# Attention into a two-layer block: the first batch's second layer takes three output chunks at once, and its weight pieces come later and closer together

## The chip, the cores and the metric

The kernel runs on one core of a Trainium2 chip. A core has a matrix engine (PE), a vector engine (DVE), a scalar engine (ACT), GpSimd (POOL) and a queue engine (SP) that here issues nearly all transfers (DMA). Each engine works through its own instructions in the order of the program; semaphores make one wait for another. The metric is the device time of one execution in microseconds (us).

## The reference

Eight batches of 12 heads with 448 positions of 64 numbers go through attention with normalized queries and keys; the result is bridged to 3584 rows of 768 and goes through two matrix products with an activation between them.

```python
q_n, k_n = (rmsnorm(q, g_q), rmsnorm(k, g_k))
scores = scale * np.matmul(q_n, k_n.transpose(0, 1, 3, 2))
attn = softmax(scores)                      # written out in the reference, with 1e-9 in the sum
x = np.matmul(attn, v)                      # then (B, H, S, D) -> (B*S, H*D)
h = x @ w_in                                # 768 -> 2048
g = h - np.tanh(h)
out = g @ w_out                             # 2048 -> 768
```

`w_in` and `w_out` arrive as float64, so the kernel reads each weight as two 32-bit words and rounds it itself.

## The kernel before

**Slots.** Attention goes by pairs of heads: six pairs in each of eight batches, 48 slots. In one slot the kernel computes the values of pair s and the scores of pair s + 1, and prepares pairs s + 2 and s + 3. Slots 0 to 5 (`first_slot`) hold attention of batch 0 alone, beside the first weights. Slots 6 to 11 (`early_slot`) hold attention of batch 1 and, woven between its parts, both layers of batch 0. From slot 12 on (`slot`) each batch's layers run beside a later batch's attention. The layers are a Python generator, `mlp`; `run(ns)` lets it emit matmuls worth so many ns between two parts of attention. In slots 6, 7 and 8 the first layer of batch 0 is emitted, 56 matmuls of 224 columns in each; in slots 9, 10 and 11 its second layer (`project_first`), 32 matmuls of 448 columns in each. One such matmul is two PE instructions in the profile.

In `early_slot` the order is: totals and two score chunks of the next pair, matmuls, the turning of a later pair's keys and queries, matmuls, the last score chunk, the values, the third score chunk, then four stretches of matmuls with the sums of exponentials, the norms and the query scaling between them. From `HALVED` on, which is slot 11, it is another: `visit` weaves the values of pair s with the scores of pair s + 1 in one block, with the score banks cut from five to three and two banks kept for the values.

**First layer.** It is done in blocks of a scheme that needs seven products where eight would be plain (`products`): four sets (j) of seven products (p, in `ORDER`), each with a weight block that is either a part of `w_in` or a sum of such parts. For batch 0 these parts are made just in time. The later batches read them back from DRAM, where the kernel keeps them.

**Pieces.** A weight piece is 128 x 768 weights, 768 KB as it arrives. Pieces 0 to 15 are `w_in`, 16 to 31 `w_out`. A piece goes through five steps on five engines: `weight_load` (L290 or L294, SP) into one of three raw buffers, `round_weight_a` (L71, L72, ACT), `round_weight_b` (L78, L79, L82, DVE), `round_weight_c` (L92, POOL), and `keep_w_out` (L388, SP), which writes some of them to DRAM. `weight(to)` emits ACT's step of the pieces below `to`, and the DVE and POOL steps of the piece before; `place_free` lets piece n be loaded only when piece n - 3 has finished on POOL. The list `due` says how many pieces must have been emitted at each of the 28 products; `combine` adds up blocks of `w_in` on DVE (L357).

**Second layer of batch 0.** `project_first` computes the six output chunks of 128 columns one after the other, 16 matmuls each, in one of three banks (`mm`). In the first three chunks it emits the last eight pieces, one in every six matmuls. In the last three chunks it emits `combine_w_out` (L381 to L384, DVE), which makes sums of `w_out` blocks for the later batches, one in every four matmuls, with their writing to DRAM (`late["keep"]`, L388). A finished chunk is copied by ACT (L1345), turned by DVE (L966) and stored by four transfers (L971), which `step_out` releases. `ring_load` brings the next batch's weight blocks into a ring of six slots.

**What the other parts do.** `norm_q` scales queries, on ACT in eight pieces (L454) for the pairs 9 to 12 and on DVE in one (L456) for others. `totals` multiplies the exponentials' sums with ones on PE (L700) and takes the reciprocal on DVE (L705); in `visit` it takes an `mm` bank, elsewhere in these slots an `sc` bank. `scores` puts two heads' scores into two `sc` banks, which are free for the next user once ACT has taken their exponentials (L575).

Of the kernel before, what the change touches and what calls it, by code (L numbers as in the profile page):

```python
# [147 lines left out]
def bounded_path(tc, ctx, q, k, v, moe_w_in, moe_w_out, out, g_col, ident, ones, half_ones, neg_half, early):  # L148
# [17 lines left out]
    nc = tc.nc  # L166
    B, H, S, D = q.shape
    DFF, DM = moe_w_out.shape
    P = 128
# [45 lines left out]
    def mm_bank():  # L215
        return bank_of("mm")
# [48 lines left out]
    def w_out_row(f, i):  # L265
        return w_half[i][f // 2][:, f % 2]
# [54 lines left out]
    def weight(to):  # L321

        while done[1] < min(to, PIECES):
            n = done[1]
            keep_step(0, {CF - 4: 0, CF: 1, CF + HF: SETS - 1}.get(n, -1))
            round_weight_a(nc, raws[n], weight_dst(n))
            settle(n)
            done[1] = n + 1
            load_weights(n + (3 if n < EARLY - 3 else 4))
            if kept[1] < kept[0] and n >= 4 * kept[0] + 2:  # L330
                keep_weights()
            keep_step(2)
        if done[1] == PIECES:
            settle(PIECES)
# [40 lines left out]
    def combine_w_out(f):  # L375

        a11, a21 = (w_out_row(f, i) for i in range(2))
        a12, a22 = (w_out_row(f + HF, i) for i in range(2))
        t = [ring_slot() for _ in range(2)]
        s3, s1, s2, s4 = (t[i // 2][:, i % 2 * HALF : (i % 2 + 1) * HALF] for i in range(4))  # L380
        nc.vector.tensor_tensor(out=s1, in0=a21, in1=a22, op=ALU.add)  # L381
        nc.vector.tensor_tensor(out=s3, in0=a11, in1=a21, op=ALU.subtract)
        nc.vector.tensor_tensor(out=s2, in0=s1, in1=a11, op=ALU.subtract)
        nc.vector.tensor_tensor(out=s4, in0=a12, in1=s2, op=ALU.subtract)  # L384
        late["keep"].append(lambda: [keep_factors(3 + 2 * i, 2, f, t[i]) for i in range(2)])

    def keep_factors(n, count, f, src):
        nc.sync.dma_start(  # L388
            out=w_out_dram[:, n : n + count, :, f, :].rearrange("p k c d -> p (k c) d"),
            in_=src[:, : count * HALF].rearrange("p (k d) -> p k d", d=P),  # L390
        )

    def keep_w_out(n):

        if not CF <= n < PIECES:
            return
        f, i, src = weight_piece(n)
        if f >= HF or i == 0:
            blk = i + 1 if f >= HF else 0
            for r in range(2):  # L400
                keep_factors(blk, 1, f % HF + r, src[:, r])
# [18 lines left out]
    def ring_load(to):  # L420

        for n in range(len(ring_tiles), min(to, len(ring_steps))):
            b, layer, j, p = ring_steps[n]
            t = ring_tiles[ring_steps[n]] = ring_slot()
            if layer == 0:
                assert kept[1] > j
                nc.sync.dma_start(out=t[:, : 2 * HALF], in_=w_in_dram[j, p])
            elif layer == 2 and p == 0:
                nc.sync.dma_start(out=t, in_=w_out_dram[:, BLOCKS[j], HC - 1].rearrange("p f d -> p (f d)"))
            elif layer == 2:  # L430
                n = min(2 * HB, 7 * HB - 2 * (p - 1) * HB)
                at = 2 * (p - 1) * HB
                nc.sync.dma_start(out=t[:, :n], in_=inner_dram[j][:, at : at + n])
            else:
                nc.sync.dma_start(out=t, in_=w_out_dram[:, BLOCKS[p], j].rearrange("p f d -> p (f d)"))
# [11 lines left out]
    def norm_q(s):  # L447
        rr, n = normed[s], early["n"]
        t = loaded.pop(("q", s))
        if NP + 3 <= s < 2 * NP + 1:  # L450
            for h in range(2):
                for c in range(NCH):
                    i = h * NCH + c
                    nc.scalar.mul(n[:, c, h], t[:, h, c], rr[:CP, 1, i : i + 1])  # L454
            return
        nc.vector.tensor_tensor(  # L456
            out=n.rearrange("p c h d -> p h c d"), in0=t,
            in1=rr[:CP, 1].rearrange("p (h c) -> p h c", h=2)[:, :, :, None].to_broadcast([CP, 2, NCH, D]),
            op=ALU.mult,
        )  # L460
# [91 lines left out]
    def sc_bank():  # L552
        return bank_of("sc")
# [93 lines left out]
    def visit(s, av):  # L647

        wave(*half_values(s, 2, av, True))
        for c in range(2):  # L650
            v0, v1 = half_values(s, c, av, False)
            if has(s + 1):
                (s0, exp0), (s1, exp1) = scores(s + 1, c, True)
                wave(s0, v1)
                exp0()
                wave(v0, s1)
                exp1()
            else:
                wave(v0, v1)
        last_values(s, av)  # L660
        del loaded["v", s]
        if s >= FOLDED:
            divide(s, av)
        if has(s + 1):
            scores(s + 1, 2)
        if s < FOLDED:
            totals(s, mm_bank())
            divide(s, av)

    def values(s, av, chunks=(2, 0, 1)):  # L670
# [14 lines left out]
    def totals(s, dn):  # L685

        parts = [t[:, h, n * HS : (n + 1) * HS] for t in sums.get(s, ()) for n in range(2) for h in range(2)]
        parts = [(parts, [ones[:, :BL]] * 2)] if parts else []
        if not sums.pop(s):
            for p in full(s):  # L690
                parts.append(
                    ([p[:, h, n * HS : (n + 1) * HS] for n in range(2) for h in range(2)], [ones[:, :BL]] * 2)
                )
            last = probs[s, KF]
            parts.append(([last[:, h, 0] for _ in range(2) for h in range(2)], [half_ones[:, n] for n in range(2)]))
        for i, (moving, by) in enumerate(parts):
            for n in range(2):
                for h in range(2):
                    r = (2 * n + h) * BL
                    nc.tensor.matmul(  # L700
                        dn[r : r + BL, :HS], lhsT=by[n], rhs=moving[2 * n + h],
                        start=(i == 0), stop=(i == len(parts) - 1),
                    )
        rs = whole[s] = sp.tile([P, HS], F32, name="rs")
        nc.vector.reciprocal(rs, dn[:, :HS])  # L705


    HALVED, FOLDED = 2 * NP - 1, 2 * NP + 1

    def fold(s):  # L710

# [100 lines left out]
    late = {}  # L812


    due = [EARLY + (CF - EARLY) * (m + 1) // (7 * SETS // 2) for m in range(7 * SETS // 2)]
    due += [CF + HF * (m + 1) // (7 * SETS // 2) for m in range(7 * SETS // 2)]
    assert len(due) == 7 * SETS and due[-1] == CF + HF

    def part(name):
        if name == "th" and "blocks" in late:  # L820
# [189 lines left out]
    def step_out(by=1):  # L1010
        for entry in late["out"]:
            entry[0] -= by
        while late["out"] and late["out"][0][0] <= 0:
            late["out"].pop(0)[1]()
# [294 lines left out]
    def project_first(b):  # L1309

        g = late["g"]
        for fn in late["todo"]:
            fn()
        late["todo"] = []
        keep_step(0, SETS - 1)
        took = 4 * S / ENGINE_NS
        for m in range(CD * CF):
            k, f = m // CF, m % CF
            n = (k + HC) % CD
            if f == 0:  # L1320
                bank = mm_bank()
            if f == CF // 2:
                step_out(2)
            if k < HC:
                weight(CF + HF + HF * (m + 1) // (HC * CF))
            elif m < HC * CF + 2:
                keep_w_out(PIECES - 2 + m - HC * CF)
            elif (m - HC * CF) % 4 == 0 and m - HC * CF <= 4 * HF:
                for fn in late["keep"]:
                    fn()  # L1330
                late["keep"] = []
                combine_w_out((m - HC * CF) // 4 - 1)
            elif m == CD * CF - 12:
                ring_load(2)
                for fn in late["keep"]:
                    fn()
            elif m == CD * CF - 10:
                ring_load(4)
            nc.tensor.matmul(  # L1339
                bank[:, :S], lhsT=w_out_row(f, n // HC)[:, n % HC * P : (n % HC + 1) * P], rhs=g[:, f, :],  # L1340
                start=(f == 0), stop=(f == CF - 1),
            )
            if f == CF - 1:
                y = part("s2").rearrange("p f s -> p (f s)")
                nc.scalar.copy(out=y, in_=bank[:, :S])  # L1345
                store(b, n, y)
            yield took
        wp_stack.close()
        late["blocks"] = pool("blocks", bufs=1)
        late["second"] = pool("second", bufs=1)  # L1350
        late["tg"] = single_stack.enter_context(tc.tile_pool(name="tg", bufs=1))
        late["inner"] = inner_steps()
# [527 lines left out]
```

## Time and profile before

| what | value |
|---|---|
| median of three runs | 1344.18 us (1344.12 to 1344.48) |
| profiled execution | 1342.53 us |
| its span, first to last instruction | 1340.7 us |
| PE, DVE, ACT, POOL busy | 1311.5, 969.5, 568.1, 795.0 us |
| mean granted PE clock | 0.998 |
| slots 6, 7, 8 (first layer of batch 0) | 36.67, 33.16, 30.28 us |
| slots 9, 10, 11 (second layer of batch 0) | 32.90, 31.70, 31.03 us |

A slot's length is taken from the start of its first PE group to that of the next slot. In a line of a timeline the columns are the start, the length, the engine, the line of the kernel, the operation, what it writes and reads, shape and count; the bracket says how long the engine had been idle before it and what ended that. A line of the waits has who waited for whom, the total in us, how often, and the longest. A busy engine is one with an instruction in flight; PE's ends are modelled, so its 98% is not 98% of its peak.

### The profile page before, as it was taken

Reading aid. Unit: us, or ns where it says so; the run is one execution under the profiler, and the core shown is the slowest. Engines: PE = TensorE matmul, PEld = TensorE weight load, DVE = VectorE, ACT = ScalarE, POOL = GpSimd, SP = SyncE. Lnnn points to the kernel's source line nnn. Section 1 sums busy time; section 2 is a strip of 40 time slices with the busy share of each in tenths; the row PEclk is TensorE's granted clock in tenths of the full one; section 3 lists DMA queues with packets and bytes.
Section 4 is the critical chain, followed back from the end, with each engine's and each line's share of the span. In section 5 each row is a group of like instructions: output and inputs, shape, how many; then the busy total and the mean of one; then the engine's idle time right before and its main releaser. Section 6 shows DMA issues by size and latency. Waiting matters only on the chain.

```text
span 1340.7 us, 29301 instructions
## 1 busy us (share of the span) xinstructions
PE 1311.5 (98%) x11368; PEld 1033.4 (77%) x11368; DVE 969.5 (72%) x1410; ACT 568.1 (42%) x1328; POOL 795.0 (59%) x591
## 2 busy tenths in 40 slices
PE   7989999999999999999999999999999999999997
PEld 3467854488998888688878788779887888799986
DVE  4999978867765767688888576768888667634455
ACT  7856654244343454445322445454512254311102
POOL 4766776348846256726698245944699244812771
PEclk9999999999999999999999999999999999999999
DMA  7779889889999766476655867466745776466544
GB/s 169 183 214 262 265 260 231 250 278 279 340 284 287 181 160 180 112 186 155 171 149 136 201 162 183 117 170 165 181 132 145 150 201 161 118 161 172 170 142 102
DMA packets 364759, 253.53 MB, mean 189 GB/s; under 512 B 273028, under 2 KB 303300, under 8 KB 364612
## 3 DMA queue, kind: packets, MB, share of 16 engines
q1 hardware_dynamic: 364608, 251.57, 69.1%
q8 instruction: 92, 1.51, 0.5%
q14 instruction: 55, 0.45, 0.1%
q10 hardware_dynamic: 4, 0.00, 0.0%
HBM read 205.23 MB, written 46.27 MB: 188 GB/s over the span
## 4 chain that ended last, share of the span: by engine, by line
PE 83%; DVE 7%; POOL 4%; DMA 2%; SPq 2%; issue 2%; ACT 1%; DVEq 0%; ACTq 0%; POOLq 0%
PE mm L857 38%; PE mm L1142 21%; PE sc L569 9%; PE sc L635 6%; PE mm L1339 5%; POOL u L1099 3%; PE sc L623 1%; POOL rr_mine L523 1%; PE sc L677 1%; DVE w_out L357 1%; PE mm L677 1%; SPq L497 1%; DVE rs L705 1%; DMA w_f<-w_inner 1%; DVE w_out L82 0%
## 5 line engine op out<-in xcount | busy, mean ns | idle before, releaser
L857 PE MATMUL mm<-xT,w_f 128*128 128x224 f32 x1296 | 263.5, 353 | 0.8 <-DVE xT L767 0.8
L857 PEld LDWEIGHTS mm<-xT,w_f 128*128 128x128 f32 x1296 | 244.8, 190 | 5.5 <-issue 4.2
L569 PE MATMUL sc<-qT,kT 64*32 64x448 f32 (+1 forms) x3072 | 215.6, 499 | 2.7 <-ACT p_last L575 2.1
L857 PE MATMUL mm<-tt,w_f 128*128 128x224 f32 x1044 | 212.6, 355 | 0.2 <-DMA w_f<-w_in 0.2
L857 PEld LDWEIGHTS mm<-tt,w_f 128*128 128x128 f32 x1044 | 195.8, 190 | 15.9 <-issue 15.4
L523 POOL TENSOR_TENSOR rr_mine<-rr_mine,neg_half 128x28 f32<-128x28 f32 x33 | 162.2, 4915 | 2.7
L762 DVE TENSOR_TENSOR xT<-xT,sc 128x448 f32<-128x448 f32 x34 | 21.0, 618 | 165.8 <-PE sc L569 114.8
L1142 PE MATMUL mm<-u,w_f 128*128 128x224 f32 x672 | 137.2, 354 | 1.0 <-POOL u L1099 0.5
L905 POOL TENSOR_TENSOR gT<-s,th 128x448 f32<-128x448 f32 x44 | 57.8, 1313 | 132.2 <-ACT th L904 128.7
L1142 PE MATMUL mm<-gT,w_f 128*128 128x224 f32 (+3 forms) x512 | 132.0, 412 | 1.2 <-DVE acc L1149 0.9
L1142 PEld LDWEIGHTS mm<-u,w_f 128*128 128x128 f32 x672 | 126.1, 190 | 8.0 <-POOL u L1099 3.6
L569 PEld LDWEIGHTS sc<-qT,kT 64*32 64x32 f32 x3072 | 72.4, 106 | 68.1 <-issue 49.2
L1142 PEld LDWEIGHTS mm<-gT,w_f 128*128 128x128 f32 x512 | 93.9, 190 | 34.3 <-issue 32.0
L635 PE MATMUL sc<-p,v_nat 64*32 64x448 f32 x1184 | 116.9, 536 | 0.0
L1142 PE MATMUL mm<-g,w_f 128*128 128x224 f32 (+1 forms) x360 | 98.9, 428 | 0.0
L575 ACT ACTIVATE p<-sc 128x448 f32<-128x448 f32 x132 | 71.9, 545 | 50.3 <-PE sc L569 37.4
L905 POOL TENSOR_TENSOR g<-s,th 128x448 f32<-128x448 f32 x24 | 30.3, 1264 | 105.1 <-ACT th L904 105.1
L1142 PEld LDWEIGHTS mm<-g,w_f 128*128 128x128 f32 x360 | 67.9, 190 | 26.5 <-issue 26.0
L729 ACT COPY sum_g<-sum 32x14 f32<-32x14 f32 x280 | 56.3, 201 | 72.0 <-DVE sum L721 66.3
L1339 PE MATMUL mm<-gT,w_out 128*128 128x448 f32 x192 | 74.0, 542 | 0.0
L145 POOL TENSOR_TENSOR rr<-rr,neg_half 112x8 f32<-112x8 f32 (+1 forms) x30 | 49.8, 1689 | 35.5 <-DVE rr L144 35.0
L1099 POOL TENSOR_TENSOR u<-gT 128x448 f32<-128x448 f32 x48 | 63.5, 1342 | 11.1 <-PE mm L1142 11.1
(206 smaller groups left out, 2465.8 us busy)
## 6 DMA issues: line engine op xcount, KB each, us to landing
w_f<-w_in SPq DMA_DIRECT2D x196, 384.0 KB, 3.5
w_f<-w_inner SPq DMA_DIRECT2D x63, 512.0 KB, 3.7
w_f<-w_out SPq DMA_DIRECT2D x42, 512.0 KB, 3.9
w_raw<-in_moe_w_out_dram SPq DMA_DIRECT2D x16, 768.0 KB, 5.4
w_in<-w_out SPq DMA_DIRECT2D x21, 384.0 KB, 5.3
qk_nat<-in_q_dram SPq DMA_DIRECT2D x132, 56.0 KB, 2.6
qk_nat<-in_k_dram SPq DMA_DIRECT2D x132, 56.0 KB, 2.4
g<-w_out SPq DMA_DIRECT2D x14, 512.0 KB, 5.4
```

The source lines that it names most:

```text
L145: nc.gpsimd.tensor_tensor(out=r, in0=r, in1=neg_half[:rows], op=ALU.pow)
L523: nc.gpsimd.tensor_tensor(out=mine, in0=mine, in1=neg_half[:, :1].to_broadcast([P, 2 * NJ]), op=ALU.pow)
L569: nc.tensor.matmul(tiles[h][i * BL : (i + 1) * BL, :n], lhsT=kT[r, c * P + at : c * P + at + BL], rhs=qT[r, first : first + n], start=True ...
L575: nc.scalar.activation(p[:, h, c if c < 2 else 0, :], tiles[h][:, :n], AF.Exp, scale=1.0 if rr is None else rr[:, 0, 2 * c + h : 2 * c + h ...
L635: nc.tensor.matmul(av[g][i * BL : (i + 1) * BL, :S], lhsT=v_nat[keys, h, c, m * BL : (m + 1) * BL], rhs=p[keys, h], start=first, stop=True ...
L677: nc.tensor.matmul(av[n][r : r + BL, :HS], lhsT=v_nat[:, h, c, m * BL : (m + 1) * BL], rhs=p[c][:, h, n * HS : (n + 1) * HS], start=False, ...
L729: nc.scalar.copy(out=acc[h * BL : (h + 1) * BL, g], in_=part[g * BL : (g + 1) * BL, h * NJ : (h + 1) * NJ])
L857: nc.tensor.matmul(bank[:, f * HS : (f + 1) * HS], lhsT=w[:, c * width + f, :], rhs=moving[p](c), start=(first and f == 0 and c == 0), sto ...
L905: eng.tensor_tensor(out=g[:, rows, cols], in0=h, in1=th, op=ALU.subtract)
L1099: nc.gpsimd.tensor_tensor(out=u[:, half], in0=a[:, half], in1=z[:, half], op=ALU.subtract)
L1142: nc.tensor.matmul(bank[:, :n], lhsT=w(i), rhs=mv, start=(first and i == 0), stop=(i == len(moving) - 1), skip_group_check=not first,)
L1339: nc.tensor.matmul(bank[:, :S], lhsT=w_out_row(f, n // HC)[:, n % HC * P : (n % HC + 1) * P], rhs=g[:, f, :], start=(f == 0), stop=(f == C ...
```

## The change

- `due` is one straight line: from 8 pieces at products 0 to 2 to 22 at product 27, where it went to 16 by product 13 and to 24 by product 27.
- `project_first` has its loops turned: it works on three chunks at once, in three banks, so that each third matmul belongs to the same chunk. The order of the halves stays.
- Ten pieces (22 to 31) are left for it. They are emitted in its first 32 matmuls, in the list `behind`.
- `combine_w_out` is emitted from matmul 24 on, one in every six matmuls, where it began at matmul 52 with one in four; for the last two of the eight, the writing to DRAM is cut into four transfers instead of two.
- Outputs are released by one step every four matmuls. The three chunks end within three matmuls, are copied into three buffers, and the third is turned into a buffer of another name.
- Ring loads are emitted at matmuls 80 and 84, where they were at 84 and 86.
- `HALVED` is slot 10, so slot 10 has the one visit too. `totals` in a visit takes an `sc` bank, since all three `mm` banks are in use.
- `norm_q` of pair 12 goes to DVE.

```diff
-        late["keep"].append(lambda: [keep_factors(3 + 2 * i, 2, f, t[i]) for i in range(2)])
+        if f < HF - 2:
+            late["keep"].append(lambda: [keep_factors(3 + 2 * i, 2, f, t[i]) for i in range(2)])
+            return
+        late["keep"].append(lambda: [keep_factors(3 + n, 1, f, s) for n, s in enumerate((s3, s1, s2, s4))])
...
-        if NP + 3 <= s < 2 * NP + 1:
+        if NP + 3 <= s < 2 * NP:
...
-            totals(s, mm_bank())
+            totals(s, sc_bank())
...
-    HALVED, FOLDED = 2 * NP - 1, 2 * NP + 1
+    HALVED, FOLDED = 2 * NP - 2, 2 * NP + 1
...
-    due = [EARLY + (CF - EARLY) * (m + 1) // (7 * SETS // 2) for m in range(7 * SETS // 2)]
-    due += [CF + HF * (m + 1) // (7 * SETS // 2) for m in range(7 * SETS // 2)]
-    assert len(due) == 7 * SETS and due[-1] == CF + HF
+    SOON_OUT, LAST_OUT = HF - 2, 32
+    due = [EARLY + (CF - EARLY + SOON_OUT) * max(m - 1, 0) // (7 * SETS - 2) for m in range(7 * SETS)]
+    behind = [min(PIECES, CF + SOON_OUT + (PIECES - CF - SOON_OUT) * (m + 1) // LAST_OUT) for m in range(CD * CF)]
+    assert due[-1] == CF + SOON_OUT and due[7 * (SETS - 1) - 1] > CF
...
-        for m in range(CD * CF):
-            k, f = m // CF, m % CF
-            n = (k + HC) % CD
-            if f == 0:
-                bank = mm_bank()
-            if f == CF // 2:
-                step_out(2)
-            if k < HC:
-                weight(CF + HF + HF * (m + 1) // (HC * CF))
-            elif m < HC * CF + 2:
-                keep_w_out(PIECES - 2 + m - HC * CF)
-            elif (m - HC * CF) % 4 == 0 and m - HC * CF <= 4 * HF:
+        combined = [0]
+
+        def keep_combined(to):
+            for f in range(combined[0], min(to, HF)):
                 for fn in late["keep"]:
                     fn()
                 late["keep"] = []
-                combine_w_out((m - HC * CF) // 4 - 1)
-            elif m == CD * CF - 12:
-                ring_load(2)
+                combine_w_out(f)
+                combined[0] = f + 1
+
+        for m in range(CD * CF):
+            k, f, i = m // (HC * CF), m % (HC * CF) // HC, m % HC
+            n = (1 - k) * HC + i
+            if m % 4 == 3:
+                step_out()
+            weight(behind[m])
+            if f == 0:
+                bank = [] if i == 0 else bank
+                bank.append(mm_bank())
+            if LAST_OUT <= m < LAST_OUT + 2:
+                keep_w_out(PIECES - 2 + m - LAST_OUT)
+            if m >= CF + HF:
+                keep_combined((m - CF - HF) // 6 + 1)
+            if m == CF + HF + 6 * HF:
                 for fn in late["keep"]:
                     fn()
-            elif m == CD * CF - 10:
+                late["keep"] = []
+            if m == CD * CF - 16:
+                ring_load(2)
+            elif m == CD * CF - 12:
                 ring_load(4)
             nc.tensor.matmul(
-                bank[:, :S], lhsT=w_out_row(f, n // HC)[:, n % HC * P : (n % HC + 1) * P], rhs=g[:, f, :],
+                bank[i][:, :S], lhsT=w_out_row(f, n // HC)[:, n % HC * P : (n % HC + 1) * P], rhs=g[:, f, :],
                 start=(f == 0), stop=(f == CF - 1),
             )
             if f == CF - 1:
-                y = part("s2").rearrange("p f s -> p (f s)")
-                nc.scalar.copy(out=y, in_=bank[:, :S])
-                store(b, n, y)
+                y = part(("s2", "s5", "s1")[i]).rearrange("p f s -> p (f s)")
+                nc.scalar.copy(out=y, in_=bank[i][:, :S])
+                store(b, n, y, part("s2").rearrange("p f s -> p (f s)") if i == 2 else None)
```

Here `NP` is 6, `CF` 16, `HF` 8, `CD` 6, `HC` 3, `SETS` 4, `EARLY` 8 and `PIECES` 32.

## The prediction, made before the change was run

> **What bounds the kernel now.** I read the page first: who is busy, and how the matrix clock stands.
>
> ```profile
> span 1340.7 us, 29301 instructions
> PE 1311.5 (98%) x11368; PEld 1033.4 (77%) x11368; DVE 969.5 (72%) x1410; ACT 568.1 (42%) x1328; POOL 795.0 (59%) x591
> ```
>
> PE is idle for 29.2 us of the span, so the change can gain only where PE stands still, or by taking work from PE. Next I cut the stretch that the change touches into slots 6 to 11, by the starts of their first PE groups, and asked for the busy time of each (us, then PE, PEld, DVE, ACT, POOL, granted clock, DMA share, GB/s):
>
> ```profile
> 72.83:109.50 36.67, 32.10 (x284) 25.99 (x277) 35.79 (x52) 19.02 (x30) 21.82 (x17) 0.95 0.84 229
> 109.50:142.66 33.16, 30.84 (x282) 25.44 (x281) 30.96 (x40) 19.82 (x37) 21.89 (x17) 1.00 0.92 261
> 142.66:172.94 30.28, 30.28 (x282) 25.50 (x281) 28.51 (x43) 18.12 (x35) 24.30 (x18) 1.00 0.84 255
> 172.90:205.80 32.90, 32.90 (x237) 16.35 (x236) 25.57 (x30) 19.79 (x36) 23.05 (x19) 1.00 0.83 258
> 205.78:237.48 31.70, 31.70 (x209) 15.55 (x209) 28.07 (x40) 15.63 (x30) 18.61 (x18) 1.00 0.95 244
> 237.48:268.51 31.03, 31.03 (x209) 15.39 (x208) 24.42 (x43) 8.08 (x15) 10.62 (x8) 1.00 0.84 245
> ```
>
> Slots 8 to 11 have no idle PE; slots 6 and 7 have 4.57 and 2.32 us, with DVE full. What PE waits for there, in the view of waits (slots 6 to 8):
>
> ```profile
> PE sc L467 <- DVE rs L705: 3.9, 2, 2.3
> PE mm L857 <- DVE s L926: 2.5, 1, 2.5
> PE mm L857 <- DVE rs L705: 0.5, 1, 0.5
> ```
>
> So DVE's backlog is the limit in slots 6 and 7, and PE alone from slot 8 on. Last, how a weight piece travels: ACT (L71, L72), DVE (L78 to L82), POOL (L92), and only then SP may load the piece three further on into the same raw buffer. One whole round, of piece 18 to piece 21, and two later waits, from the timeline (start, us):
>
> ```profile
> 152.00 0.90 ACT L71 ACTIVATE w_out<-w_raw 128x768 f32<-128x768 f32 x1
> 152.94 0.56 DVE L78 TENSOR_SCALAR w_out<-w_out 128x768 f32<-128x768 f32 x1 [0.41 <-ACT w_out L71]
> 156.05 2.62 POOL L92 TENSOR_TENSOR w_out<-w_out,w_raw 128x384 int32<-128x384 int32 x2
> 158.71 0.38 SPq L294 DMA_DIRECT2D w_raw<-in_moe_w_out_dram  x1
> 164.49 0.92 ACT L71 ACTIVATE w_out<-w_raw 128x768 f32<-128x768 f32 x1 [1.03 <-DMA w_raw<-in_moe_w_out_dram]
> ...
> 206.28 0.96 ACT L71 ACTIVATE w_out<-w_raw 128x768 f32<-128x768 f32 x1 [5.39 <-DMA w_raw<-in_moe_w_out_dram]
> ...
> 210.32 2.18 ACT L575 ACTIVATE p<-sc,rr 128x448 f32<-128x448 f32 x4
> ...
> 221.52 0.95 ACT L71 ACTIVATE w_out<-w_raw 128x768 f32<-128x768 f32 x1 [3.07 <-DMA w_raw<-in_moe_w_out_dram]
> ```
>
> The round takes 164.49 - 152.00 = 12.5 us, the shortest that I found: 4.2 us a piece. Piece 28 (206.28) stood 5.39 us for its load, and the exponentials of scores finished at 207.97 waited behind it until 210.32. The last piece, 31, starts at 221.52.
>
> [...] exponentials sit behind a conversion whose load is late. [...] Here the 2.55 us stall at 88.60 was followed by granted clocks of 0.60 for 2.85 us and 0.81 for 3.00 us, which is 0.4 x 2.85 + 0.19 x 3.00 = 1.7 us lost; the 2.32 us stall at 118.4 lost nothing. [...] the DVE part of a piece took 0.56 + 0.56 + 0.96 = 2.1 us alone and 0.97 + 1.25 + 1.66 = 3.9 us beside POOL at 155.53.
>
> **The change, part by part.**
>
> *Pieces in the first layer.* Due counts before: 8 to 16 over the first 14 products, to 24 over the next 14. After: a straight line from 8 to 22. Products 0 and 1 settle pieces 6 and 7 in both, and the s5 addition (L926) behind them stays: slot 6's three stalls remain, gain 0. By product 9 (start of slot 7) two pieces and three combinations fewer stand before slot 7's reciprocal: 2 x 2.1 + 3 x 0.9 = 6.9 us at least, while that reciprocal ran 119.09 - 111.5 = 7.6 us late. The pow and the query scaling ahead of slot 8's exponentials come earlier by a like amount. So the 2.32 us stall goes: -2.3. Between nothing and 2.9 (slot 7's excess over slot 8). Slots 7 and 8 still hold ten pieces, with three combinations more, 3 us of DVE that the vanished backlog pays for.
>
> *One visit from slot 10.* Slot 10 (31.70) becomes like slot 11 (31.03): -0.7. The scores get three banks instead of five there, and totals take the bank of the last exponential of chunk 1: in slot 11 that ended at 242.59 and totals began at 242.91, so 0, at worst 0.3 each in slots 10 to 12. Query scaling of slot 12 moves from ACT (2.02) to DVE (0.65): 0.
>
> *Pieces in 32 matmuls.* This is where it is decided. Let T = 0 be the start of slot 9. Before, pieces 24 to 31 are spread over 48 matmuls, and the last starts at T = 221.52 - 172.94 = 48.6. After, ten pieces, 22 to 31, are issued at matmuls 3, 6, 9, 12, 15, 19, 22, 25, 28, 31, all inside slot 9. ACT takes them in order, with attention's exponentials behind. PE would reach the exponentials that follow piece 26 (the third score chunk of slot 10, which reuses the bank of the last-chunk scores) at totals 1.65 + scores 1.67 + turn 0.83 + 16 matmuls x 0.766 + 0.40 + 0.51 + 2.41 = 19.7. It would reach those behind piece 31 (second wave of the new slot 10 visit) at 32.8 + 1.9 = 34.7.
> When can ACT be through? Piece 22 stands behind slot 9's first exponentials: pow done at 2.3, scaling 2.0, exponentials 2.2, one tanh 0.55: it starts at 7.1. Piece 31 is three rounds later: 7.1 + 3 x 12.5 = 44.6, plus its own two ACT operations 1.74 and the first exponential 0.4: 46.7. PE stands 46.7 - 34.7 = 12.0 us in all. Part of it comes early: piece 23 starts at about 10 (POOL done with piece 20 at 4.4, load 5.4), piece 26 at 22.5, its exponential is done at 24.6, so 4.9 us in slot 9, and the other 7.1 in slot 10. Both are longer than the stall that cost 1.7 us of clock: +3.4.
> Bounds: the smallest landing (4.5) with the smallest stages (1.74 + 2.1 + 2.0 + 0.3) gives rounds of 10.6 and a loss of 6.3; a round of 14 gives 16.5. I take 12.5 because it was measured, with DMA as busy as it will be.
>
> *Three banks at once, combinations from matmul 24, split keeps.* PE's 192 instructions stay. Bank 0 is refilled two matmuls (1.53 us) after its end, and its ACT copy takes 0.53: 0, covered by an ACT that has only 8.08 us of work in 31.03; uncovered it would be 0.5 per turn. Combinations add 2 x 2.2 us of DVE to slot 9 and leave slots 10 and 11: in the sum of a rival below. The two split keeps add four DMA issues at about 0.5 us on SP, after the last raw load: 0. Ring loads come at matmuls 80 and 84 instead of 84 and 86: 0. At the end three stores instead of one are followed by 12 output DMAs where 4 were; SP then has eight more issues of about 0.6 us before the ring loads of slot 12. The seventh ring load was issued at 283.29 for a product at about 289, with landings of 3.5 to 5.6: 0, at worst 2. Output steps every fourth matmul: 0.
>
> Sum: -2.3 - 0.7 + 12.0 + 3.4 = +12.4. The profiled execution has 1342.53 with 1.83 outside its span, and the runs' median is 1344.18: I add the sum to either. Span 1353.1, median 1344.18 + 12.4 = **1356.6**.
>
> **Rivals.**
> *Loads keep up* (ends faster). If ACT is through piece 31 by T = 34.7, nothing is lost and 3.0 is gained: 1341.2. For it: slot 9 used 0.83 of the DMA time, in bursts of up to 418 GB/s in the DMA view. Against: a round would have to fall below (34.7 - 0.4 - 1.74 - 7.1) / 3 = 8.5 us, under the smallest stages' sum of 10.6.
> *DVE becomes the bound in slot 9.* Its 25.6 us there gain five pieces (10.5 to 19), two combinations (4.4 to 8) and the scaling 0.65, less one store: 40 to 52 us against 32.8 of PE. Pieces then queue at DVE, with sums and norms between them, and rounds grow to 15 or more: 7.1 + 45 + 2.1 - 34.7 = 19.5, median 1364. For it: piece 28 would have the sums and the first combination before it; against: ACT's waits leave DVE free early in the slot.
> *A small loss.* ACT is early by chance at slot 9, rounds near 10.6, and one stall too short to cool the clock: 6.3 + 0 - 3.0 = +3.3, 1347.5.
>
> **How the numbers follow.** Main case 0.62 (own range 1349.5 to 1362), DVE bound 0.10, small loss 0.10 (half of it above 1346.9), loads keep up 0.18. One measurement can tell 0.2%, 2.7 us, from no change: 1341.5 to 1346.9 is the same. Faster 0.17, within 0.06, slower 0.77. Range 1341 to 1366: it leaves out about 0.09 below and 0.05 above.
>
> **What would show it.** Slot 7's wait on the reciprocal is gone and the slot lasts about 30.5. In slot 9 PE waits for ACT's exponentials (L575) about 5 us before the third score chunk, and in slot 10 about 7 us inside the visit. ACT waits for raw loads in most of pieces 25 to 31, with the last piece near T = 45, and the clock drops twice. If ACT is through at T = 35, or PE's waits stay under 1 us, the main step is wrong; if DVE holds the pieces while their loads have landed, the second rival is right.

## The result, and the profile after

The median goes from 1344.12 us (five runs, 1342.81 to 1344.48) to 1359.94 us (five runs, 1357.98 to 1360.79): a ratio of 1.0114, with 1.0100 to 1.0128 as its 95% interval. The change costs some 15.8 us. The profiled execution of after took 1360.79 us and has a span of 1358.9 us, 18.2 more than the one of before. It is the slowest of its five runs, and the one of before (1342.53) was faster than each of its five, so some two us of the 18.2 are the difference between executions.

First the page of after: span and engines.

```profile
span 1358.9 us, 29306 instructions
PE 1315.8 (97%) x11368; PEld 1034.7 (76%) x11368; DVE 974.8 (72%) x1412; ACT 567.4 (42%) x1321; POOL 789.9 (58%) x591
```

PE has the same 11368 matmuls and is busy 4.3 us longer. It is idle for 1358.9 - 1315.8 = 43.1 us, where it was 29.2. So 13.9 us of the 18.2 are standing still, and 3.1 of the other 4.3 are the same matmuls at a lower clock, as is worked out below. Where that happens is seen in the same table by slots as for before, slots 6 to 11:

```profile
73.30:110.33 37.03, 32.45 (x296) 25.88 (x285) 33.67 (x49) 19.36 (x31) 20.40 (x16) 0.95 0.69 192
110.33:140.30 29.97, 29.97 (x281) 25.39 (x280) 27.46 (x39) 17.52 (x34) 21.54 (x16) 1.00 0.88 255
140.30:170.27 29.97, 29.97 (x281) 25.39 (x280) 28.09 (x42) 20.78 (x38) 20.53 (x16) 1.00 0.91 298
170.27:213.67 43.40, 35.27 (x233) 16.87 (x232) 38.62 (x42) 22.73 (x39) 29.36 (x25) 0.92 0.90 263
213.67:253.60 39.93, 33.52 (x209) 16.60 (x208) 35.93 (x55) 11.83 (x20) 17.62 (x16) 0.91 0.86 230
253.60:284.64 31.04, 31.04 (x210) 15.40 (x209) 14.44 (x22) 8.07 (x15) 8.59 (x7) 1.00 0.48 143
```

Slot 7 falls from 33.16 to 29.97 us and slot 8 from 30.28 to 29.97: these two gain 3.5 (slot 6 is 0.4 longer). Slot 9 grows from 32.90 to 43.40 and slot 10 from 31.70 to 39.93. Slot 11, which has the three banks at once and the visit, is 31.04 where it was 31.03. The waits of PE for exponentials in slots 6 to 11, which are new, and the two of them in the timeline (the scores' matmul is L572 here and was L569, the exponential L578 and was L575):

```profile
PE sc L572 <- ACT p_last L578: 14.5, 2, 8.1
```

```profile
199.04 1.74 PE L572 MATMUL sc<-qT,kT 64*32 64x448 f32 x14 [8.13 <-ACT p_last L578]
...
222.90 0.95 PE L572 MATMUL sc<-qT,kT 64*32 64x448 f32 x1 [6.41 <-ACT p_last L578]
```

Two score groups wait for a bank whose exponential ACT has not taken. ACT is busy for only 22.73 us of slot 9, so it is not overworked. Its own timeline shows what it stands for:

```profile
196.97 0.89 ACT L71 ACTIVATE w_out<-w_raw 128x768 f32<-128x768 f32 x1 [3.80 <-DMA w_raw<-in_moe_w_out_dram]
...
198.56 0.76 ACT L578 ACTIVATE p_last<-sc,rr 128x224 f32<-128x224 f32 x2
...
220.83 0.90 ACT L71 ACTIVATE w_out<-w_raw 128x768 f32<-128x768 f32 x1 [4.09 <-DMA w_raw<-in_moe_w_out_dram]
...
222.41 0.77 ACT L578 ACTIVATE p_last<-sc,rr 128x224 f32<-128x224 f32 x2
```

The piece at 196.97 is 26, and the one at 220.83 is 31, the last. Each time ACT stands for a load with nothing to do, converts the piece, and takes the exponential next; PE goes on 0.5 us later. The exponential at 198.56 had its scores since about 187.3 and still ran after the conversion, though ACT stood idle for 1.80 and 3.80 us in between. So a weight load ends PE's wait, through a queue in which the exponential stands behind the conversion.

The clock is low after both waits: granted 0.54 over the 3.46 us from 199.04 on and 0.50 over the 3.10 us from 222.90 on. That is 0.46 x 3.46 + 0.50 x 3.10 = 3.1 us of full speed lost. Slot 9 with its wait taken out is 43.40 - 8.13 = 35.27, 2.4 more than before's 32.90; slot 10 is 39.93 - 6.41 = 33.52, 2.5 more than an undisturbed slot of its kind (31.03). Together these are 4.9 us, 1.8 more than the clock explains. The rest is lost at the stop itself. The group of matmuls in which slot 9's wait stands, its first part in after and then the whole group in before:

```profile
189.97 0.94 PE L572 MATMUL sc<-qT,kT 64*32 64x448 f32 x2
```

```profile
192.64 0.98 PE L569 MATMUL sc<-qT,kT 64*32 64x448 f32 x16
```

Sixteen of these overlap and take 0.98 us. In after two of them are issued before the wait, and they take 0.94 us by themselves. PE counts as busy in that time, but it gets little done. So the idle time of a stop understates what it costs, here by some 0.9 us for each of the two.

The sum: slots 9 to 11 +18.7, slots 7 and 8 -3.5, the front up to slot 7 +0.8, the rest of the span +2.1. The last is two waits of PE for ring loads, some 75 and 165 us after slot 11, which the profile of before doesn't have (waits of PE from 290 us on):

```profile
PE mm L861 <- DMA w_f<-w_in: 2.2, 2, 1.3
```

### The profile page after: what moved, and what is told of

It reads as the page before. It is cut to its first block, busy times and chain, and to the rows that moved or that the text cites. A ratio compares the mean times of both kernels' runs of the same rounds, so it can differ in the third digit from the quotient of the medians.

```text
span 1358.9 us, 29306 instructions
## 1 busy us (share of the span) xinstructions
PE 1315.8 (97%) x11368; PEld 1034.7 (76%) x11368; DVE 974.8 (72%) x1412; ACT 567.4 (42%) x1321; POOL 789.9 (58%) x591
## 4 chain that ended last, share of the span: by engine, by line
PE 79%; DVE 6%; POOL 4%; DMA 4%; SPq 2%; issue 2%; ACT 1%; ACTq 0%; DVEq 0%; POOLq 0%
PE mm L861 38%; PE mm L1146 20%; PE sc L572 8%; PE sc L638 6%; PE mm L1352 4%; POOL u L1103 2%; DMA w_raw<-in_moe_w_out_dram 1%; PE sc L626 1%; DMA w_f<-w_in 1%; DMA w_raw<-in_moe_w_in_dram 1%; POOL rr_mine L526 1%; PE mm L680 1%; DVE w_out L82 1%; SPq L127 1%; SPq L290 1%
## 5 line engine op out<-in xcount | busy, mean ns | idle before, releaser
L572 PE MATMUL sc<-qT,kT 64*32 64x448 f32 (+1 forms) x3072 | 219.8, 503 | 17.1 <-ACT p_last L578 16.5
L572 PEld LDWEIGHTS sc<-qT,kT 64*32 64x32 f32 x3072 | 73.7, 107 | 83.6 <-issue 49.6
L638 PE MATMUL sc<-p,v_nat 64*32 64x448 f32 x1216 | 122.6, 542 | 0.0
L578 ACT ACTIVATE p<-sc 128x448 f32<-128x448 f32 x132 | 71.9, 545 | 50.3 <-PE sc L572 37.4
L638 PEld LDWEIGHTS sc<-p,v_nat 64*32 64x32 f32 x1216 | 45.1, 108 | 33.9 <-issue 33.4
```

What stands on the lines that cost most here:

```text
L572: nc.tensor.matmul(tiles[h][i * BL : (i + 1) * BL, :n], lhsT=kT[r, c * P + at : c * P + at + BL], rhs=qT[r, first : first + n], start=True ...
L578: nc.scalar.activation(p[:, h, c if c < 2 else 0, :], tiles[h][:, :n], AF.Exp, scale=1.0 if rr is None else rr[:, 0, 2 * c + h : 2 * c + h ...
L638: nc.tensor.matmul(av[g][i * BL : (i + 1) * BL, :S], lhsT=v_nat[keys, h, c, m * BL : (m + 1) * BL], rhs=p[keys, h], start=first, stop=True ...
```

## The experiments

The kernel before ran beside each group of experiments on the same chip: 1343.38 us in experiments 1 to 4, 1342.89 in 5 to 8, 1342.98 in 9 to 11. I call a median's distance from it the excess; that of after is 15.8 us. To compare executions without the rest of the kernel I also give for some kernels the stretch from slot 9's first totals to slot 11's totals, which is 69.97 us in before (172.94 to 242.91) and 88.76 in after (170.27 to 259.03). Of its 18.8 us, 14.5 are the two waits and 4.9 the low clock and the stops themselves, less the 0.7 of the visit.

**1. Pieces nearly as slow as they were: ten in 48 matmuls.**

```diff
-    SOON_OUT, LAST_OUT = HF - 2, 32
+    SOON_OUT, LAST_OUT = HF - 2, 48
```

> The changed kernel with its ten last pieces spread over 48 matmuls of the second layer instead of 32 (one in 4.8 instead of 3.2), nothing else. Theory (a raw buffer comes free once in a round of about 12.5 us, so three buffers carry one piece in 4.2 us; ACT's queue hands the delay to PE): 4.8 matmuls with their share of attention last about 4.8 us, so the two waits of PE for the exponentials of the last chunk, 14.5 us in all, fall under 1 us together, the clock is back at 0.998, and the median is 1341 to 1343. Rival, the turned loop with all three banks costs the time: 1355 or more. Rival, the combinations from matmul 24 on overload DVE: 1350 or more.

The median is 1354.79 us, a ratio of 1.0091 (1.0077 to 1.0105): an excess of 11.4 us, so only 4.4 come back. The waits for exponentials are gone, as the theory said, but the time went into a new wait, which I had priced at nothing. PE in slots 9 to 11, from the waits:

```profile
PE mm L1352 <- ACT s L1358: 10.5, 2, 8.5
```

And what ACT does meanwhile:

```profile
226.31 0.90 ACT L71 ACTIVATE w_out<-w_raw 128x768 f32<-128x768 f32 x1 [8.17 <-DMA w_raw<-in_moe_w_out_dram]
...
227.90 0.94 ACT L1358 COPY s<-mm 128x448 f32<-128x448 f32 x2
231.74 0.91 ACT L71 ACTIVATE w_out<-w_raw 128x768 f32<-128x768 f32 x1 [2.90 <-DMA w_raw<-in_moe_w_out_dram]
...
233.34 0.52 ACT L1358 COPY s<-mm 128x448 f32<-128x448 f32 x1
```

Matmul 48 opens the next three chunks in the banks of the first three. Those banks are free when ACT has copied them. The copies are emitted at matmuls 45 to 47, behind pieces 30 and 31 (emitted at matmuls 43 and 47), whose loads are late. With one chunk after the other a finished bank had 32 matmuls before it was needed again; with three at once it has two. So the pace of the pieces and the three banks belong together: pieces that outlast matmul 48 hit the copies, and faster ones hit the exponentials.

**2. Combinations late, nearly as they were.** This asks whether DVE's load in slot 9 is the bound, as the prediction's second rival said.

```diff
-            if m >= CF + HF:
-                keep_combined((m - CF - HF) // 6 + 1)
-            if m == CF + HF + 6 * HF:
+            if m >= HC * CF:
+                keep_combined((m - HC * CF) // 4 + 1)
+            if m == HC * CF + 4 * HF:
```

> The changed kernel with the combinations of blocks from matmul 48 on, one in every four, as before; the ten pieces stay in the first 32 matmuls. Theory: both waits stay, 13 to 15 us together, median 1357 to 1361. Rival, DVE is the bound in slots 9 and 10: the combinations' 4 to 8 us leave slot 9, so the waits shrink to half, median 1346 to 1352.

The median is 1357.48 us (ratio 1.0109, 1.0093 to 1.0125), an excess of 14.1. The two waits stay, 12.3 us together and so a little less than I gave, in slot 9 a little longer and in slot 10 shorter. From the timeline of PE:

```profile
197.35 1.74 PE L572 MATMUL sc<-qT,kT 64*32 64x448 f32 x14 [8.99 <-ACT p_last L578]
...
218.91 0.76 PE L572 MATMUL sc<-qT,kT 64*32 64x448 f32 x1 [3.34 <-ACT p_last L578]
```

DVE is not the bound, but it has a share. In after, piece 28 leaves ACT at 205.25 and its DVE part starts at 211.61, because the sums and the first combination stand before it:

```profile
208.83 1.26 DVE L381 TENSOR_TENSOR w_f<-w_out,w_out 128x384 f32<-128x384 f32 x1
...
211.61 0.55 DVE L78 TENSOR_SCALAR w_out<-w_out 128x768 f32<-128x768 f32 x1
```

Piece 31 may be loaded only when piece 28 is through, so this combination, which takes 2.9 us, would account for most of the 3.1 us by which slot 10's wait shrinks without it.

**3. Seven raw buffers.** Five of the last eight pieces (24 to 27 and 31) are loaded into slots of the weight ring, which is not in use then. A load then waits for the piece seven places back, and not for the third. The combinations are late as in experiment 2, so that the buffers alone differ from it.

```diff
+        elif 24 <= n < 28 or n == 31:
+            raw = ring[:, (n - 24) % 7 * 2 * DM : ((n - 24) % 7 + 1) * 2 * DM].bitcast(I32)
...
-        return n - 3 < max(done[2], EARLY)
+        return n - (7 if n >= 24 else 3) < max(done[2], EARLY)
...
-            load_weights(n + (3 if n < EARLY - 3 else 4))
+            load_weights(n + (3 if n < EARLY - 3 else 8 if n >= 20 else 4))
```

> As the kernel with late combinations, and pieces 24 to 27 and 31 are loaded into the ring, which is empty until the combinations begin, so seven raw buffers serve pieces 24 to 31 and their loads are issued ahead. Theory, the wait is for a raw buffer to come free: the two waits fall under 2 us together, median 1341 to 1345. Rival, the bandwidth of DMA or the work of DVE and POOL on ten pieces is the bound: the waits stay above 8 us, median 1352 or more.

The median is 1348.03 us (ratio 1.0034, 1.0022 to 1.0046), 9.5 less than experiment 2. The waits for exponentials fall from 12.3 to 1.9 us. That is the buffer round shown: the same pieces at the same matmuls through the same engines, with earlier loads. The median stays above what I expected, since another wait of 3.0 us for a query scaling on DVE appears in slot 10 (PE, slots 9 to 11):

```profile
PE sc L476 <- DVE n L461: 3.0, 1, 3.0
PE sc L574 <- ACT p_last L580: 1.9, 1, 1.9
```

This profile also has 3.1 us of waits for ring loads after slot 11.

**4. The pace alone, in the kernel before.** Its eight pieces come at the pace of the change (ten in 32 matmuls), with the chunks one by one and the old order of slot 10.

```diff
-                weight(CF + HF + HF * (m + 1) // (HC * CF))
+                weight(min(PIECES, CF + HF + 10 * (m + 1) // 32))
```

> The kernel before with only its last eight pieces pressed into one in 3.2 matmuls (26 instead of 48); loop, banks, first layer, combinations and slot 10 as before. Theory: PE waits about 10 us in slot 9 for the exponentials of the last chunk, behind pieces 24 to 28 on ACT, and median is 1352 to 1358. Rival, the turned loop, the earlier visit or the combinations are the cause: 1343 to 1346.

The median is 1360.1 us (ratio 1.0123, 1.0107 to 1.0138), an excess of 16.7: a loss as large as the change's, without its other parts, and above what I gave. Its wait is one of 13.2 us, all in slot 9, where I had about 10:

```profile
206.87 1.74 PE L569 MATMUL sc<-qT,kT 64*32 64x448 f32 x14 [13.16 <-ACT p_last L575]
```

**5. 56 matmuls.** If the copies only have to be clear of the last two pieces, a still slower pace might avoid both waits. Here the combination of one block reads a piece that is not yet rounded, so that part of the output is another; no work is left out.

```diff
-    SOON_OUT, LAST_OUT = HF - 2, 32
+    SOON_OUT, LAST_OUT = HF - 2, 56
```

> The changed kernel with its ten last pieces over 56 matmuls, so that the last two are emitted after the ACT copies of the three finished banks (matmuls 45 to 47) and no longer before them; nothing else. Theory (over 48 matmuls PE waited 10.5 us for these copies, since the three banks leave no spare and the copies stood on ACT behind pieces whose loads were late): waits for exponentials and for copies fall under 2 us together, median 1341 to 1344. Rival, three chunks in all three banks cost this at their end wherever the pieces are: the wait for the copies stays above 7 us, median 1350 or more.

The median is 1351.19 us (ratio 1.0059, 1.0046 to 1.0071). The copies still wait, now behind piece 29, which is emitted at matmul 44, and PE waits 6.8 us for them (timeline of ACT):

```profile
226.03 0.90 ACT L71 ACTIVATE w_out<-w_raw 128x768 f32<-128x768 f32 x1 [8.58 <-DMA w_raw<-in_moe_w_out_dram]
...
227.61 1.38 ACT L1358 COPY s<-mm 128x448 f32<-128x448 f32 x3
```

So the rival was right, but for 0.2 us of its wait: it is not which piece stands before the copies, but that any late one does.

**6. The new first layer in the kernel before.** Only the list of due pieces is changed; pieces 22 and 23 follow at matmuls 1 and 4 of the second layer, and the rest as before.

```diff
-    due = [EARLY + (CF - EARLY) * (m + 1) // (7 * SETS // 2) for m in range(7 * SETS // 2)]
-    due += [CF + HF * (m + 1) // (7 * SETS // 2) for m in range(7 * SETS // 2)]
+    SOON_OUT = HF - 2
+    due = [EARLY + (CF - EARLY + SOON_OUT) * max(m - 1, 0) // (7 * SETS - 2) for m in range(7 * SETS)]
...
-                weight(CF + HF + HF * (m + 1) // (HC * CF))
+                weight(CF + HF + HF * (m + 1) // (HC * CF) if m >= 8 else CF + SOON_OUT + (m >= 1) + (m >= 4))
```

> The kernel before with the changed list for the first layer (22 pieces by its end instead of 24); the two pieces that are left are emitted at matmuls 1 and 4 of the second layer, and pieces 24 to 31 as before, one in six. Chunks one by one, visit from slot 11. Theory: slot 7 is 3 us shorter, as in the changed kernel, and slot 9 has ACT late by at most 2 us, mostly covered: median 1.5 to 3 us below the kernel before. Rival, two more pieces at the head of slot 9 are enough to bring the wait for exponentials: 2 us or more above it.

The median is 1342.32 us over 21 runs, a ratio of 1.0001 (0.9993 to 1.0008): no change, which neither the theory nor the rival had. Slots 7 and 8 take 29.97 us each, as in after, but slot 9 takes 36.8 where it took 32.9. The first chunk goes through all its 16 blocks in the first 16 matmuls, and needs pieces 22 and 23 before they are rounded (PE, slots 9 to 11):

```profile
PE mm L1339 <- POOL w_out L92: 2.3, 3, 1.1
```

The gain of the first layer is real and given back in slot 9. Three chunks at once need each block three times later, which is what turning the loops is good for.

**7. Seven buffers and 40 matmuls together.** Pieces end before the copies (matmul 40 before 45), the buffers let them come at that pace, and the combinations follow from matmul 44 on, one in four.

```diff
-    SOON_OUT, LAST_OUT = HF - 2, 32
+    SOON_OUT, LAST_OUT = HF - 2, 40
...
-            if m >= CF + HF:
-                keep_combined((m - CF - HF) // 6 + 1)
-            if m == CF + HF + 6 * HF:
+            if m >= HC * CF - 4:
+                keep_combined((m - HC * CF + 4) // 4 + 1)
+            if m == HC * CF - 4 + 4 * HF:
```

(and the three edits of experiment 3)

> The kernel with seven raw buffers and late combinations, its pieces over 40 matmuls instead of 32 and the combinations from matmul 44 on. Theory: with 32 what was left were 1.9 us for exponentials behind the last piece and 3.0 us for a scaling on DVE behind ten pieces; at 40 both fall under 1 us, and the median is 1340 to 1343, below the kernel before. Rival, DVE and POOL cannot carry ten pieces in this stretch: 1346 or more.

The median is 1339.21 us, a ratio of 0.9971 (0.9960 to 0.9982): below both kernels, if only by 3.7 us against before. From slot 9's totals to slot 11's totals (same columns as the table by slots):

```profile
167.42:237.00 69.58, 69.36 (x569) 34.16 (x569) 66.89 (x76) 38.82 (x67) 46.48 (x39) 1.00 0.80 241
```

PE is idle for 0.22 us of 69.58 and keeps its full clock. All that the change was to gain is there; the stretch takes 0.4 us less than in before, and slots 7 and 8 keep their gain.

**8. The visit in slot 10, without the change's faster pieces.** Experiment 6 with the visit from slot 10 on.

```diff
-            totals(s, mm_bank())
+            totals(s, sc_bank())
...
-    HALVED, FOLDED = 2 * NP - 1, 2 * NP + 1
+    HALVED, FOLDED = 2 * NP - 2, 2 * NP + 1
```

(and the edits of experiment 6)

> As the kernel before with the changed list for the first layer, and with the one visit from slot 10 on and totals in a score bank, both as in the changed kernel. Theory: slot 10 is another 0.7 us shorter, median 0.5 to 1 us below the run with the list alone. Rival, three score banks in slot 10 bring a new wait: 0.3 us or more above it.

The median is 1347.15 us (ratio 1.0035, 1.0022 to 1.0049), 4.8 more than experiment 6, where I had 0.7 less. PE waits 2.9 us in slot 10, inside the visit, for an exponential that ACT had not taken; what kept ACT is not shown here. The clock is 0.50 for the 2.9 us after it:

```profile
212.09 0.95 PE L569 MATMUL sc<-qT,kT 64*32 64x448 f32 x1 [2.88 <-ACT p_last L575]
```

The visit asks for its first exponentials 1.9 us after its slot begins. In these runs it gains only where ACT is on time.

**9. 40 matmuls with three buffers.** This parts the two halves of experiment 7.

```diff
-    SOON_OUT, LAST_OUT = HF - 2, 32
+    SOON_OUT, LAST_OUT = HF - 2, 40
```

> The kernel after with its ten pieces spread over 40 matmuls instead of 32, three raw buffers as before, combinations where the change has them. It tells pace from buffers in the run that had both (seven buffers and 40 matmuls, 1339.2). My theory: PE's wait for the ACT copies of the three banks stays away (the last piece is emitted at matmul 39, before the copies at 45 to 47, and ACT is through it before PE comes to matmul 48), but the exponentials still stand behind late pieces, 5 to 8 us in the two slots together, since a round of 12.5 us over three buffers still makes 4.2 us a piece; median 1347 to 1351. If the pace alone was the cause, no such wait is left and the median is 1339 to 1343.

The median is 1347.19 us (ratio 1.0038, 1.0025 to 1.0052). The copies make no wait, as expected; the exponentials make 4.2 us, a little under what I gave (waits of PE, the two are 2.70 us in slot 9 and 1.48 in slot 10):

```profile
PE sc L572 <- ACT p_last L578: 4.2, 2, 2.7
```

The excess is 4.2. So eight matmuls more are worth 11.6 us of after's 15.8, and the buffers with the later combinations another 7.9 (to -3.7 in experiment 7); which of these two does it was not parted. The stretch takes 77.04 us here against 69.58, with PE busy 72.86 against 69.36. Of these 3.5 us 1.7 are the clock (0.77 over the 2.05 us from 191.55 on, 0.50 over the next 2.40, 0.99 over the 2.00 after them). The other 1.8 are as much as two stops took in after beside their idle time and the clock.

**10. After, with the old order in slot 10.**

```diff
-    HALVED, FOLDED = 2 * NP - 2, 2 * NP + 1
+    HALVED, FOLDED = 2 * NP - 1, 2 * NP + 1
```

> The kernel after, with the one visit from slot 11 on as in the kernel before, so that slot 10 has the older order again; the rest of the change stays. My theory: the visit asks for the exponentials early in slot 10, so the 6.4 us wait of that slot goes or falls under 2, while the 8.1 us wait of slot 9 stays; median 1351 to 1354. Rival: ACT's lateness is only handed on, PE waits as long in slot 10 at another place (6 us or more), and the median stays at 1358 to 1361.

The median is 1361.34 us (ratio 1.0137, 1.0122 to 1.0153), an excess of 18.4: the rival was right, and 0.3 us short. Slot 9's wait stays at 8.3 us. That of slot 10 is not the visit's doing. It is handed on to the turning of a later pair, which uses a bank that the totals hold until their reciprocal has run, and that reciprocal stands on DVE behind a combination and the last pieces (the DVE part of one runs until 226.56, a scaling until 227.15). PE, then DVE, one timeline each:

```profile
228.80 1.11 PE L470 MATMUL sc<-ident,qk_nat 128*128 128x128 f32 x4 [6.72 <-DVE rs L708]
```

```profile
227.18 1.56 DVE L708 RECIPROCAL rs<-sc 128x224 f32<-128x224 f32 x1
```

**11. Experiment 7 with the old order in slot 10.** The edit is that of experiment 10.

> The kernel with seven raw buffers and 40 matmuls (1339.2), with the one visit from slot 11 on instead of slot 10. It measures what the visit in slot 10 is worth when ACT is not late. Prediction's step: the visit saves 0.7 us, so this kernel takes 0.7 more, 1339.9, hardly to be told from 1339.2. Rival: the visit costs or gains more than 2 us even then, and the median is under 1337 or above 1341.5.

The median is 1342.12 us over 22 runs (ratio 0.9991, 0.9983 to 0.9999), an excess of -0.9, 2.8 above that of experiment 7. So the visit in slot 10 is worth more than the 0.7 of the prediction when ACT is on time. The stretch takes 72.02 us against 69.58, 2.4 more. In it PE waits twice for DVE in slot 10, 0.42 us for the sums (0.22 with the visit) and 0.85 for the reciprocal (none with the visit), and is busy 1.4 us longer. This profile also has 2.5 us of waits for ring loads after slot 11, which that of experiment 7 doesn't have, so the medians' 2.8 need not be the visit's alone.

## Why the prediction was right, and where it was not

The main case came true: its place, its mechanism and its sign. The forecast of 1356.6 us is 3.3 under the median, and the range holds it. That it came so near is luck in part, since its terms err both ways: the pieces' term was some 6 us too small, one clock term of 1.7 us was counted twice, and slots 7 and 8 gained 1.2 us more than forecast.

**Pieces in 32 matmuls: right, and under-sized.** The prediction had 12.0 us of PE standing, 4.9 in slot 9 before the third score chunk and 7.1 inside slot 10's visit. The trace has 8.13 and 6.41 at just these two places, 14.5 in all. The term that was too small is the round of the three raw buffers, 12.5 us "because it was measured". From piece 22 (175.55) to piece 31 (220.83) there are three rounds in 45.3 us, 15.1 each, and piece 31 starts at T = 50.6 where 44.6 was forecast. Piece 22 itself started at T = 5.3 instead of 7.1, so the rounds' excess of 7.8 us came to 6.0. The 12.5 was the shortest round seen, in slot 8, and its load was issued as soon as POOL had finished (158.71). Two causes can be read off. The round from piece 23 to 26 takes 16.5 us: 8.9 until POOL has finished (189.36), then 2.6 on SP's queue, then a landing of 5.0. SP could not issue the load because it was busy with three groups of transfers for attention and one that keeps a rounded piece:

```profile
186.81 0.94 SPq L103 DMA_DIRECT2D qk_nat<-in_q_dram  x2
...
190.15 1.62 SPq L391 DMA_DIRECT2D w_out<-w_out  x2
191.94 0.37 SPq L294 DMA_DIRECT2D w_raw<-in_moe_w_out_dram  x1
```

The prediction had no term for a busy SP queue ahead of the pieces' loads. The last round, from piece 28 to 31, takes 17.3 us with the first combination in it (experiment 2). Both lie above the upper bound of 14 that the prediction gave the round, so that bound was wrong, too. Experiments 3 and 4 carry the mechanism: more buffers take the waits from 12.3 to 1.9 us, and the pace alone brings such a loss into the kernel before. One reading that the prediction leaned on was loose: in before, the exponentials of 210.32 stood right behind a copy (207.98) and a query scaling of 2.02 us (208.40), which piece 28 had made late, and not right behind the piece.

**Clock: 3.4 forecast and 3.1 measured, but counted once too often, and the stops themselves left out.** The prediction took 1.7 us for each stall; by the same working they cost 1.6 and 1.55. But its 12.0 us, 46.7 - 34.7, are all that PE is late when it goes on in the visit, and what slot 9's clock loses is inside them: a PE that comes later to the visit waits less there. The sum should have added the second stall's clock alone. In after PE goes on in the visit at T = 222.90 - 170.27 = 52.6, which is 17.9 us behind 34.7: 14.5 for the two waits, 1.6 for slot 9's clock, and 1.8 for the two stops beside their idle time, for which the prediction had no term.

**Slot 7's stall: -2.3 forecast, -3.2 measured.** The slot lasts 29.97 us, not 30.5, and slot 8 gains 0.3. The working named 2.9, slot 7's excess over slot 8, as the end of what it could be; it was the better value. The idle 2.32 us leave 0.9 of the 3.2 out; that these are the stop itself, here too, is an estimate from the 0.9 us a stop in after. Experiment 6 shows the same 29.97 with this part alone.

**One visit in slot 10: -0.7 was wrong as a fixed sum.** As work of PE the step was about right: in experiment 7, with hardly any wait, PE is busy for 69.36 us of the stretch where before has 69.97. But experiments 8 and 11 give +4.8 and -2.8 for the same edit. The step asked what the visit saves on PE and left out that it changes when PE asks for ACT and DVE: earlier for exponentials, later for the reciprocal. That the loss would be handed on without the visit (experiment 10) I had not expected either.

**Three banks at once: 0 was right for this kernel and for a reason that doesn't carry.** After has no wait for the copies. But the working named as cover an ACT with only 8.08 us of work in slot 11, and 0.5 us a turn without it. The cover was of the wrong kind: what matters is not how busy ACT is but what stands before the copy in its queue. Uncovered it cost 10.5 us (experiment 1) and 6.8 (experiment 5). In after the last piece has left ACT at 222.5 (T = 52.2), before PE goes on in slot 10, so nothing late stands before the copies. Without the waits PE would have come to matmul 48 at about T = 51.8 (an estimate: 32.8 for slot 9 and 18.9 from the start of before's slot 11 to its sixteenth large matmul), so the margin was small.

**Ring loads and output transfers: "0, at worst 2".** Ring waits of 2.2 us did come, but not before slot 12, where the working looked. They are far later, experiment 6 has 1.4 us of them without three banks or their transfers, and the profiles of experiments 1, 4 and 7 have none. So the step's mechanism isn't shown; what causes them stays open.

**Totals in an `sc` bank, split keeps, query scaling:** nothing in the trace speaks against their 0. Slot 11 is 31.04 us.

**The rivals.** Loads do not keep up: ACT waits for them before eight pieces of slots 8 to 10. DVE is not the bound, but the second rival had the right detail in it: a combination ahead of a piece can be read as most of 3 us in slot 10. The small loss needed rounds of 10.6, and none of those followed here was under 12.0.

## What to carry to other kernels

Where a conversion fed by a transfer stands in an engine's queue ahead of work that PE needs, its price is not its busy time (here 1.7 us of ACT a piece) but how late its load is (here waits of PE of 8.13 and 6.41 us): count the round of its buffers (every engine in it, and the queue that issues the load), and compare it with the pace at which you emit the pieces. Take the round from a stretch as crowded as the new one will be, and not the shortest. Before filling all accumulator banks at once, look at what stands in front of their copies: a bank that was free for 32 matmuls and now has two of slack takes over the delays of that queue (10.5 us in experiment 1). And when you price a wait, add what the stop costs beside its idle time (here some 0.9 us), and count a delay that an earlier stall already contains only once.

## What the runs showed of the hardware that was not expected

How long a stall must be to cool PE's clock was not a fixed number in these runs. The stall in slot 6 from which the prediction took its 1.7 us is in every profile, 2.5 us long. In before, after and experiments 4 and 8 the eight matmuls behind it take 2.81, 2.45, 2.03 and 2.64 us, and the granted clock in after is 0.66 and then 0.77 over two stretches of 3 us; in experiments 1, 3, 5, 6 and 7 they take 1.78. These matmuls in after and then in experiment 6:

```profile
92.03 2.45 PE L861 MATMUL mm<-xT,w_out 128*128 128x224 f32 x8 [2.54 <-DVE s L930]
```

```profile
91.94 1.78 PE L857 MATMUL mm<-xT,w_out 128*128 128x224 f32 x8 [2.54 <-DVE s L926]
```

So the 1.7 us are there in one execution and not in the next. Within one execution it is no different. A stall of 1.90 us in slot 10 of experiment 3 was followed by a granted clock of 0.53, while one of 3.01 us later left it at 1.00 (same columns as the table by slots):

```profile
205.42:208.50 3.08, 3.08 (x39) 1.86 (x47) 2.98 (x5) 1.45 (x3) 0.94 (x2) 0.53 0.72 209
220.91:224.00 3.09, 3.09 (x12) 1.79 (x13) 2.99 (x5) 1.58 (x3) 2.32 (x3) 1.00 0.76 202
```

The clock was low behind stalls of 2.88 us (experiment 8: 0.50 over 2.91 us) and 2.70 us (experiment 9), too. Those of 1.48 us (experiment 9) and 2.32 us (before) left it at 1.00, over the 2.31 and 3.30 us behind them. The drop can come after PE has gone on: behind the 2.70 us in experiment 9 PE is busy again from 191.55, and the granted clock is 0.77 over the first 2.05 us and 0.50 over the next 2.40. What decides whether a stall cools the clock these runs do not show.
